# Grouped-query attention and a gated MLP: one fixed order for all engines, six score bursts a batch, a ring of PSUM banks, and DMA transposes

## The chip, the cores and the metric

The kernel runs on one NeuronCore of a Trainium2 chip. The metric is the time of one execution in microseconds (us), as the device measures it. The spans of the profiles here are 1 to 2 us shorter than the times of the same executions.

Names: PE or TensorE is the matrix engine (PEld its weight loads), DVE is VectorE, ACT is ScalarE, POOL is GpSimd, SP issues DMAs. PSUM is the memory that matmuls write; both kernels divide it into eight banks, each of 512 fp32 numbers (2 KB) per partition. A score unit is one pair of score matmuls with its exponential, and a burst is the score matmuls of one visit, one after another.

## The reference

Eight batches, 384 positions, 16 query heads and 4 key/value heads of 64. Attention without a mask, then a feed-forward part whose gate mixes positions:

```python
scores = q @ k.T / sqrt(64)                  # each kv head serves 4 query heads
x      = softmax(scores) @ v                 # -> (8, 384, 1024)
h      = relu(x @ w_in)                      # w_in 1024 x 1024
u, v   = h[..., :512], h[..., 512:]
v_n    = (v - mean(v)) / sqrt(var(v) + 1e-6) # over the 512
v_s    = w_spatial @ v_n + b_spatial         # mixes the 384 positions
out    = (u * v_s) @ w_out                   # 512 -> 1024
```

## The kernel before

Matmuls run in fp16 with fp32 sums. Scores are computed transposed (keys on partitions), in pairs of 64-row matmuls for two kv heads; ScalarE takes the exponential; the sums of the softmax and the products with v are 32-column matmuls, four at a time on the array (in the trace twelve of them take 0.49 us, as long as three full ones of 163 ns). The reciprocal is `exp(-ln(sum))` on ScalarE, and VectorE multiplies. `mk_v`, `mk_u`, `mk_sp` and `mk_out` below are the feed-forward groups V, U, spatial and O.

The order of PE, POOL and SP was fixed by hand; that of VectorE and ScalarE was left to the scheduler. Each batch has nine visits of two score units, and after each visit as many feed-forward groups of the batch before as a time budget allows. PSUM was two pools: four banks for scores, four for all else.

```python
    ps_sc = ctx.enter_context(tc.tile_pool(name="ps_sc", bufs=2, space=bass.MemoryType.PSUM))
    ps = ctx.enter_context(tc.tile_pool(name="ps", bufs=4, space=bass.MemoryType.PSUM))
# ... (cut)
    def transpose_q(b, gp, jp):          # and the same for k: TensorE, then a VectorE copy
        # ... (cut)
                nc.tensor.transpose(pq[:, jj, t, :], q16[:, t, 2 * jp + jj, :, :].rearrange("p h d -> p (h d)"), ident16)
        nc.vector.tensor_copy(qT[b, gp][:, 2 * jp : 2 * jp + 2, :, :], pq)
# ... (cut)
    def mk_sp(b, m):
        # ... (cut)
            nc.tensor.matmul(psp[:, 0:S], bias_ones, bias_rows, start=True, stop=False)   # the bias
            for st in range(NST):
                nc.tensor.matmul(psp[:, 0:S], held["v_n", b, st][:, m * P : (m + 1) * P], wsT16[:, st, :],
                                 start=False, stop=(st == NST - 1))
            nc.vector.tensor_tensor(held["gT", b][:, m, :], psp[:, 0:S], held["uT", b][:, m, :], ALU.mult)
# ... (cut)
    VISITS = 9
    VALUES_AT = {0: (-1, 1, 1), 3: (0, 0, 0), 5: (0, 0, 1), 8: (0, 1, 0)}
    # ... (cut)
    with tc.manual_schedule(engines={PE, POOL, SP}):
        # ... (cut)
                if b < B:
                    scores(b, [2 * vi, 2 * vi + 1])
                if vi in VALUES_AT:
                    # ... (cut)
                        values(b + db, gp, quad)
                # ... (cut)
                budget += per_visit
                while queue and (b == B or done < budget):
                    t, f = queue.pop(0)
                    f()
                    done += t
```

The softmax here doesn't subtract the row's maximum and nothing guards it: scores larger than these inputs give would overflow.

Of the kernel before, what the change touches and what calls it, by code (L numbers as in the profile page):

```python
# [14 lines left out]
PE, POOL, SP = mybir.EngineType.PE, mybir.EngineType.Pool, mybir.EngineType.SP  # L15
# [3 lines left out]
def kernel(  # L19
# [11 lines left out]








    nc = tc.nc
    P = 128  # L40
# [10 lines left out]
    NGP = HKV // 2  # L51
    assert S == NST * P and DM == NKT * P and DH == 512 and D == 64 and G == 4
    assert HQ * D == DM and G * S == 3 * 512 and NST == 3 and NGP == 2
# [5 lines left out]
    wpool = ctx.enter_context(tc.tile_pool(name="wpool", bufs=1))  # L59
    stage = ctx.enter_context(tc.tile_pool(name="stage", bufs=1))  # L60
    ld = ctx.enter_context(tc.tile_pool(name="ld", bufs=1))
    qk16 = ctx.enter_context(tc.tile_pool(name="qk16", bufs=2))
    tr_sb = ctx.enter_context(tc.tile_pool(name="tr_sb", bufs=3))
    att_a = ctx.enter_context(tc.tile_pool(name="att_a", bufs=2))
    xt_pool = ctx.enter_context(tc.tile_pool(name="xt_pool", bufs=3))
    r_pool = ctx.enter_context(tc.tile_pool(name="r_pool", bufs=3))
    moe_sb = ctx.enter_context(tc.tile_pool(name="moe_sb", bufs=2))
    moe_v = ctx.enter_context(tc.tile_pool(name="moe_v", bufs=6))
    small = ctx.enter_context(tc.tile_pool(name="small", bufs=4))
    out_pool = ctx.enter_context(tc.tile_pool(name="out_pool", bufs=3))  # L70

    ps_sc = ctx.enter_context(tc.tile_pool(name="ps_sc", bufs=2, space=bass.MemoryType.PSUM))
    ps = ctx.enter_context(tc.tile_pool(name="ps", bufs=4, space=bass.MemoryType.PSUM))
# [15 lines left out]
    loaded = {}  # L89

    def load_k(b):
        k32 = ld.tile([P, HKV, NST * D], FP32, name=f"k32_{b}", tag="k32")
        nc.sync.dma_start(k32, k[b].rearrange("g (p t) d -> p g (t d)", t=NST))
        loaded["k32", b] = k32

    def load_v(b):
        v32 = ld.tile([P, HKV, NST * D], FP32, name=f"v32_{b}", tag="v32")
        nc.sync.dma_start(v32, v[b].rearrange("g (p t) d -> p g (t d)", t=NST))
        loaded["v32", b] = v32

    def load_q(b, gp, pieces=1):
        q32 = ld.tile([P, 2 * G, NST * D], FP32, name=f"q32_{b}_{gp}", tag=f"q32_{gp}")
        n = 2 * G // pieces
        for i in range(pieces):
            h0 = gp * 2 * G + i * n
            nc.sync.dma_start(
                q32[:, i * n : (i + 1) * n, :],
                q[b, h0 : h0 + n].rearrange("h (p t) d -> p h (t d)", t=NST),
            )
        loaded["q32", b, gp] = q32  # L110

    def cast_k(b, engine):
        k16 = qk16.tile([P, NST, HKV, D], FP16, name=f"k16_{b}", tag="k16")
        engine.tensor_copy(k16, loaded["k32", b].rearrange("p g (t d) -> p t g d", t=NST))  # L114
        loaded["k16", b] = k16

    def cast_v(b, engine):
        v16 = qk16.tile([P, HKV, NST, D], FP16, name=f"v16_{b}", tag="v16", bufs=3)
        engine.tensor_copy(v16.rearrange("p g t d -> p g (t d)"), loaded["v32", b])
        loaded["v16", b] = v16  # L120

    def cast_q(b, gp, engine):
        q16 = qk16.tile([P, NST, G, 2, D], FP16, name=f"q16_{b}_{gp}", tag=f"q16_{gp}")
        q32 = loaded["q32", b, gp]
        for half in range(2):
            engine.tensor_copy(
                q16[:, :, :, half, :],
                q32[:, half * G : (half + 1) * G, :].rearrange("p j (t d) -> p t j d", t=NST),
            )
        loaded["q16", b, gp] = q16  # L130

    def load_batch(b, first):
        load_k(b)
        load_q(b, 0)
        cast_k(b, first)
        cast_q(b, 0, first)
        load_v(b)
        load_q(b, 1)
        cast_v(b, nc.gpsimd)
        cast_q(b, 1, nc.gpsimd)  # L140
# [6 lines left out]
    bias_rows = cst.tile([P, S], FP16, name="bias_rows")  # L147
    bias_ones = cst.tile([P, P], FP16, name="bias_ones")
    w_in16 = wpool.tile([P, NKT, DFF], FP16, name="w_in16")
    w_out16 = wpool.tile([P, NDT, DM], FP16, name="w_out16")  # L150
    wsT16 = wpool.tile([P, NST, S], FP16, name="wsT16")

    def load_consts():
        make_identity(nc, ident)
        nc.vector.tensor_copy(ident16, ident)  # L155
        nc.vector.memset(ones32, 1.0)
        nc.vector.memset(eps_t, eps_ln)
        nc.vector.memset(bias_rows, 0.0)
        nc.vector.memset(bias_ones, 0.0)
        nc.vector.memset(bias_ones[0:1, :], 1.0)  # L160
        nc.vector.memset(bias_ones[32:33, :], 1.0)

    def load_bias():
        b32 = cst.tile([1, S], FP32, name="b32")
        lo32 = cst.tile([1, NST, P], FP32, name="lo32")
        nc.sync.dma_start(b32, moe_b_spatial.rearrange("(a s) -> a s", a=1))
        b_tp = b32.rearrange("a (p t) -> a t p", t=NST)
        hi = bias_rows[0:1, :].rearrange("a (t p) -> a t p", t=NST)
        lo = bias_rows[32:33, :].rearrange("a (t p) -> a t p", t=NST)
        nc.vector.tensor_copy(hi, b_tp)  # L170
        nc.vector.tensor_tensor(lo32, b_tp, hi, ALU.subtract)
        nc.vector.tensor_copy(lo, lo32)

    def load_w_in(c0, c1):

        for gp in range(2):
            for half in range(2):
                for quad in range(2):
                    r0 = (gp * 2 * G + half * G + 2 * quad) * D
                    rows = moe_w_in[r0 : r0 + 2 * D, c0:c1].rearrange(  # L180
                        "(jq jj r) n -> jq r jj n", jq=2, jj=2
                    )
                    kc = gp * 4 + quad * 2
                    for jq in range(2):
                        i = half * 2 + jq
                        nc.gpsimd.dma_start(  # L186
                            w_in16[32 * i : 32 * (i + 1), kc : kc + 2, c0:c1], rows[jq]
                        )
# [8 lines left out]
    def load_ws():  # L197
        ws32 = stage.tile([P, NST, S], FP32, name="ws32", tag="ws32", bufs=1)
        nc.sync.dma_start(ws32, moe_w_spatial.rearrange("(p tt) s -> p tt s", tt=NST))
        ws16 = stage.tile([P, NST, NST, P], FP16, name="ws16", tag="ws16", bufs=1)  # L200
        for tt in range(NST):
            nc.vector.tensor_copy(  # L202
                ws16[:, tt, :, :], ws32[:, tt, :].rearrange("p (s t) -> p t s", t=NST)
            )
        loaded["ws16"] = ws16

    def transpose_ws(st):
        ws16 = loaded["ws16"]
        psw = ps.tile([P, NST, P], FP16, name=f"psw_{st}", tag="ps")
        for tt in range(NST):  # L210
            nc.tensor.transpose(psw[:, tt, :], ws16[:, tt, st, :], ident16)
        nc.vector.tensor_copy(wsT16[:, st, :].rearrange("p (t q) -> p t q", t=NST), psw)


    kT, qT, aT, xT = {}, {}, {}, {}

    def transpose_k(b):
        k16 = loaded[("k16", b)]
        pk = ps.tile([P, NGP, NST, P], FP16, name=f"pk_{b}", tag="ps")
        for gp in range(NGP):  # L220
            for t in range(NST):
                nc.tensor.transpose(  # L222
                    pk[:, gp, t, :],
                    k16[:, t, 2 * gp : 2 * gp + 2, :].rearrange("p g d -> p (g d)"),
                    ident16,
                )
        kT[b] = tr_sb.tile([P, NGP, NST, P], FP16, name=f"kT_{b}", tag="kT")
        nc.vector.tensor_copy(kT[b], pk)

    def transpose_q(b, gp, jp):  # L230
        q16 = loaded[("q16", b, gp)]
        if jp == 0:
            qT[b, gp] = tr_sb.tile([P, G, NST, P], FP16, name=f"qT_{b}_{gp}", tag=f"qT_{gp}", bufs=2)
        pq = ps.tile([P, 2, NST, P], FP16, name=f"pq_{b}_{gp}_{jp}", tag="ps")
        for jj in range(2):
            for t in range(NST):
                nc.tensor.transpose(
                    pq[:, jj, t, :],
                    q16[:, t, 2 * jp + jj, :, :].rearrange("p h d -> p (h d)"),
                    ident16,  # L240
                )
        nc.vector.tensor_copy(qT[b, gp][:, 2 * jp : 2 * jp + 2, :, :], pq)

    def scores(b, units):
        scs = []
        for u in units:
            gp, c, t = u // 9, (u % 9) // 3, u % 3
            sc = ps_sc.tile([P, 2, 512], FP32, name=f"sc_{b}_{u}", tag="sc")
            rhs = qT[b, gp].rearrange("p j t q -> p (j t q)")
# [19 lines left out]
    def values(b, gp, quad):  # L269
# [23 lines left out]
        for jj in range(2):  # L293
# [4 lines left out]
            )  # L298


    held = {}

    def mk_v(b, st):
        def f():
# [203 lines left out]
```

## Time and profile before

Two runs took 301.69 and 302.72 us. From the page of the profile: the span, the busy time of each engine, and the engines' shares of the chain of waits (the chain of work that ended last, followed back from the end; "issue" in it is time for which the profile shows no wait, and SPq is SP's instruction queue).

```profile
span 301.4 us, 5836 instructions
PE 269.2 (89%) x2457; PEld 125.4 (42%) x2457; DVE 161.7 (54%) x310; ACT 184.3 (61%) x249; POOL 53.2 (18%) x82
...
PE 69%; ACT 16%; DMA 6%; DVE 4%; issue 2%; SPq 1%; POOL 0%; DVEq 0%
```

The next view gives busy time in four stretches, cut where a batch's first score matmul starts: before batch 1, batch 1, batches 2 to 6, batch 7 with the tail. PEclk is the granted clock of TensorE, as a share of full speed; the DMA share is the summed time of all DMA packets over that of 16 engines. It passes 1 where packets overlap.

```profile
core 0: us, PE busy (x) PEld busy (x) DVE busy (x) ACT busy (x) POOL busy (x), PEclk, DMA share, GB/s
0.00:35.05 35.05, 18.52 (x192) 9.00 (x193) 15.63 (x30) 20.51 (x25) 20.00 (x41) 0.90 0.99 240
35.05:72.38 37.33, 34.36 (x314) 16.08 (x313) 19.19 (x38) 23.40 (x32) 8.69 (x12) 0.95 0.38 94
72.38:243.39 171.01, 163.87 (x1533) 75.73 (x1532) 94.24 (x181) 114.26 (x155) 24.54 (x30) 1.00 0.36 116
243.39:301.40 58.01, 52.41 (x425) 24.60 (x424) 32.64 (x63) 26.16 (x38) 0.00 (x0) 0.99 0.16 65
```

A steady batch takes 171.01 / 5 = 34.2 us. PE is busy for 96% of that, ScalarE for 67%, VectorE for 55%. The timeline of one steady batch shows what PE does and what its steps cost: start, duration, engine, line, operation, output and inputs.

```profile
99.90 0.51 PE L237 MATMUL pq_0_0_1339<-ident_102,q_3_0_1062 128*128 128x128 f16 x6
...
101.97 1.03 PE L387 MATMUL po_1_1_1361<-w_out_108,gT_1281 128*128 128x512 f16 x4
...
102.93 0.39 PE L252 MATMUL sc_16_1368<-qT_1_1031,kT_831 64*128 64x512 f16 x2
...
103.15 0.38 PE L252 MATMUL sc_17_1371<-qT_1_1031,kT_831 64*128 64x512 f16 x2
...
103.46 0.67 PE L280 MATMUL sums_1_0_1376<-aT_1_1197,ones_103 128*32 128x384 f16 x12
```

A record lasts longer than the step to the next one: the matmuls of O take 379 ns each, and a group of four starts 0.86 us after the group before it (101.11 and 101.97). So what is counted here is the step from start to start. Between records of matmuls that follow each other the median step is 216 ns for 512 columns, 163 ns for 384, 56 ns for a transpose (its copy, on VectorE, takes 0.55 us for each 128x768), about 0.22 us for a pair of 64-row score matmuls (102.93 to 103.15) and 0.49 us for twelve 32-column ones. Where the shape of the array changes (a mode change, below), a step is longer: from O to scores 312 ns (216 would do), from scores to sums 306, from the 32-column groups to full ones 258 (163 would do). That is some 95 ns for each change.

So a batch is, in us: scores 4.0, sums and values 5.9, V 5.2, U 5.2, spatial with bias 2.6, O 5.2, transposes 1.7, together 29.8; mode changes 22 x 0.095 = 2.1; the remaining 2.3 of 34.2 are waits.

### The profile page before, as it was taken

Reading aid. Unit: us, or ns where it says so; the run is one execution under the profiler, and the core shown is the slowest. Engines: PE = TensorE matmul, PEld = TensorE weight load, DVE = VectorE, ACT = ScalarE, POOL = GpSimd, SP = SyncE. Lnnn points to the kernel's source line nnn. Section 1 sums busy time; section 2 is a strip of 40 time slices with the busy share of each in tenths; the row PEclk is TensorE's granted clock in tenths of the full one; section 3 lists DMA queues with packets and bytes.
Section 4 is the critical chain, followed back from the end, with each engine's and each line's share of the span. In section 5 each row is a group of like instructions: output and inputs, shape, how many; then the busy total and the mean of one; then the engine's idle time right before and its main releaser. Section 6 shows DMA issues by size and latency. Waiting matters only on the chain.

```text
span 301.4 us, 5836 instructions
## 1 busy us (share of the span) xinstructions
PE 269.2 (89%) x2457; PEld 125.4 (42%) x2457; DVE 161.7 (54%) x310; ACT 184.3 (61%) x249; POOL 53.2 (18%) x82
## 2 busy tenths in 40 slices
PE   0576879899899989999899989999899989999993
PEld 0332434444445434444345434444344434444551
DVE  3437325564465554665455654755455754645574
ACT  1396965657776585566786485566876485675300
POOL 0666952000140003200050001500051000000000
PEclk9977979999999999999999999999999999999998
DMA  7999991003660219103570219103480111003105
GB/s 216 315 287 218 116 254 35 2 0 142 197 188 2 119 52 318 37 0 141 164 222 0 103 50 316 56 2 140 137 251 0 70 73 72 0 2 139 72 0 209
DMA packets 31852, 35.57 MB, mean 118 GB/s; under 512 B 1489, under 2 KB 28114, under 8 KB 31826
## 3 DMA queue, kind: packets, MB, share of 16 engines
q1 hardware_dynamic: 28722, 32.05, 32.4%
q0 software_dynamic: 3104, 3.15, 6.8%
q8 instruction: 19, 0.31, 0.4%
q14 instruction: 7, 0.06, 0.1%
HBM read 25.76 MB, written 12.58 MB: 127 GB/s over the span
## 4 chain that ended last, share of the span: by engine, by line
PE 69%; ACT 16%; DMA 6%; DVE 4%; issue 2%; SPq 1%; POOL 0%; DVEq 0%
DMA ws_316<-in_moe_w_spatial_dram 3%; DMA q_0_1_135<-in_q_dram 3%; ACT aT_1_720 L265 1%; ACT aT_0_2385 L265 1%; ACT aT_0_969 L265 1%; ACT aT_1_335 L265 1%; ACT aT_0_1441 L265 1%; ACT aT_0_489 L265 1%; PE pv_0_588 L311 1%; ACT aT_0_3329 L265 1%; ACT aT_0_1913 L265 1%; ACT aT_0_2857 L265 1%; ACT aT_1_2613 L265 1%; ACT aT_1_3539 L265 1%; ACT aT_1_3085 L265 1%
## 5 line engine op out<-in xcount | busy, mean ns | idle before, releaser
L348 PEld LDWEIGHTS <-w_in_107 128*128 128x128 f16 x256 | 23.9, 98 | 21.6 <-issue 6.9
L186 POOL DMA_DIRECT2D w_in_107<-in_moe_w_in_dram x32 | 17.1, 543 | 5.3 <-DMA w_in_107<-in_moe_w_in_dram 5.3
L280 PEld LDWEIGHTS <-ones_103 128*32 128x32 f16 x384 | 7.4, 96 | 15.1 <-issue 13.3
L222 PE MATMUL pk_177<-ident_102,k_0_128 128*128 128x128 f16 x6 | 0.8, 303 | 9.6 <-DVE ident_102 L155 9.6
L265 ACT ACTIVATE aT_0_209<-sc_0_203 128x1024 f16<-128x1024 f32 x1 | 1.0, 1024 | 10.3 <-PE sc_0_203 L252 10.3
L114 POOL CAST k_3_1060<-k_3_1056 128x768 f16<-128x768 f32 x1 | 0.8, 827 | 33.0 <-DVE stats_0_1086 L321 33.0
L252 PEld LDWEIGHTS <-kT_184 64*128 64x128 f16 x36 | 2.1, 99 | 9.4 <-issue 8.9
L114 POOL CAST k_6_2476<-k_6_2472 128x768 f16<-128x768 f32 x1 | 0.8, 827 | 27.7 <-DMA k_6_2472<-in_k_dram 27.7
L114 POOL CAST k_5_2004<-k_5_2000 128x768 f16<-128x768 f32 x1 | 0.8, 827 | 26.6 <-DMA k_5_2000<-in_k_dram 26.6
L114 POOL CAST k_7_2948<-k_7_2944 128x768 f16<-128x768 f32 x1 | 0.8, 827 | 25.4 <-DMA k_7_2944<-in_k_dram 25.4
L114 POOL CAST k_4_1532<-k_4_1528 128x768 f16<-128x768 f32 x1 | 0.8, 827 | 25.1 <-DMA k_4_1528<-in_k_dram 25.1
L280 PEld LDWEIGHTS <-v_0_138 128*32 128x32 f16 x96 | 2.9, 106 | 4.4 <-issue 3.2
L202 DVE CAST ws_318<-ws_316 128x384 f16<-128x384 f32 x3 | 1.9, 671 | 5.2 <-DMA ws_316<-in_moe_w_spatial_dram 5.2
L222 PEld LDWEIGHTS <-k_0_128 128*128 128x128 f16 x6 | 0.6, 133 | 9.5 <-DVE k_0_128 L114 5.2
L364 PEld LDWEIGHTS <-bias_ones 128*128 128x128 f16 x32 | 3.1, 97 | 3.5 <-issue 2.3
L311 PEld LDWEIGHTS <-xt_271 128*128 128x128 f16 x24 | 2.7, 116 | 3.5 <-issue 1.6
L387 PEld LDWEIGHTS <-gT_3623 128*128 128x128 f16 x24 | 2.2, 98 | 3.5 <-issue 0.7
L387 PEld LDWEIGHTS <-gT_3895 128*128 128x128 f16 x24 | 2.3, 98 | 3.0 <-DVE gT_3895 L373 0.5
L387 PEld LDWEIGHTS <-gT_2697 128*128 128x128 f16 x24 | 2.2, 97 | 3.0 <-DVE gT_2697 L373 0.6
L387 PEld LDWEIGHTS <-gT_1753 128*128 128x128 f16 x24 | 2.2, 97 | 3.0 <-DVE gT_1753 L373 0.6
L387 PEld LDWEIGHTS <-gT_2225 128*128 128x128 f16 x24 | 2.2, 97 | 3.0 <-DVE gT_2225 L373 0.6
L387 PEld LDWEIGHTS <-gT_1281 128*128 128x128 f16 x24 | 2.2, 97 | 3.0 <-DVE gT_1281 L373 0.6
(1168 smaller groups left out, 804.7 us busy)
## 6 DMA issues: line engine op xcount, KB each, us to landing
w_in_107<-in_moe_w_in_dram POOLq DMA_DIRECT2D x32, 64.0 KB, 5.4
w_out_108<-in_moe_w_out_dram POOLq DMA_DIRECT2D x2, 512.0 KB, 7.4
q_0_0_125<-in_q_dram SPq DMA_DIRECT2D x2, 384.0 KB, 5.4
q_0_1_135<-in_q_dram SPq DMA_DIRECT2D x2, 384.0 KB, 8.3
q_1_0_247<-in_q_dram SPq DMA_DIRECT2D x1, 768.0 KB, 6.2
q_1_1_256<-in_q_dram SPq DMA_DIRECT2D x1, 768.0 KB, 8.5
q_2_0_571<-in_q_dram SPq DMA_DIRECT2D x1, 768.0 KB, 12.9
q_2_1_580<-in_q_dram SPq DMA_DIRECT2D x1, 768.0 KB, 8.2
```

The lines of the kernel that those rows point to most:

```text
L114: engine.tensor_copy(k16, loaded["k32", b].rearrange("p g (t d) -> p t g d", t=NST))
L186: nc.gpsimd.dma_start(w_in16[32 * i : 32 * (i + 1), kc : kc + 2, c0:c1], rows[jq])
L202: nc.vector.tensor_copy(ws16[:, tt, :, :], ws32[:, tt, :].rearrange("p (s t) -> p t s", t=NST))
L222: nc.tensor.transpose(pk[:, gp, t, :], k16[:, t, 2 * gp : 2 * gp + 2, :].rearrange("p g d -> p (g d)"), ident16,)
L252: nc.tensor.matmul(sc[:, half, :], kT[b][lo:hi, gp, t, :], rhs[lo:hi, c * 512 : (c + 1) * 512], start=True, stop=True,)
L265: nc.scalar.activation(aT[b, gp][:, t, :, c * 512 : (c + 1) * 512], sc, AF.Exp, scale=scale)
L280: nc.tensor.matmul(dst[32 * i : 32 * (i + 1), 0:S], weights(t, half), a[:, t, half, j * S : (j + 1) * S], start=(t == 0), stop=(t == NST - 1),
L311: nc.tensor.matmul(pv, xt[:, kc, st * P : (st + 1) * P], w_in16[:, kc, DH:DFF], start=(kc == 0), stop=(kc == NKT - 1),)
L348: nc.tensor.matmul(pu[:, 0:S], w_in16[:, kc, mu * P : (mu + 1) * P], xT[b][:, kc, :], start=(kc == 0), stop=(kc == NKT - 1),)
L364: nc.tensor.matmul(psp[:, 0:S], bias_ones, bias_rows, start=True, stop=False)
L387: nc.tensor.matmul(po, gT[:, m, tt * P : (tt + 1) * P], w_out16[:, m, half * 512 : (half + 1) * 512], start=(m == 0), stop=(m == NDT - 1),)
```

## The change

Its intent: fix the order of all engines; have fewer changes of the array's shape (six bursts of three score units in place of nine of two, and the softmax sums and values of two head groups together); take the transposes off TensorE (a DMA transposes, batch 0 excepted); fuse the gate (the bias becomes an addition on VectorE, and ReLU and gate one VectorE instruction; V's ReLU moves from ScalarE to VectorE); let every group use every PSUM bank (the free one used longest ago); start sooner; and do the first half of batch 0's V and U in batch 0. The feed-forward is also spread over two batches: V and half of spatial and U one batch later, the other half and O two batches later. The core of the diff:

```diff
-    ps_sc = ctx.enter_context(tc.tile_pool(name="ps_sc", bufs=2, space=bass.MemoryType.PSUM))
-    ps = ctx.enter_context(tc.tile_pool(name="ps", bufs=4, space=bass.MemoryType.PSUM))
+    psp = ctx.enter_context(tc.tile_pool(name="psp", bufs=1, space=bass.MemoryType.PSUM))
+    banks = psp.tile([P, 8, 512], FP32, name="banks")
+    def take1():
+        x = min((i for i in range(8) if not busy[i]), key=lambda i: used[i])
+        mark(True, (x,))
+        return x
 # ... (cut: take2 takes a pair in the same way; touch() marks a bank as free after its last reader)
+    def turn_q_dma(b, gp):
+        nc.sync.dma_start_transpose(
+            new_qT(b, gp).rearrange("p a b c -> p (a b) c"),
+            T["q16", b, gp].rearrange("p j t h d -> p (j t h d)"),
+        )
 # ... (cut)
-            nc.tensor.matmul(psp[:, 0:S], bias_ones, bias_rows, start=True, stop=False)
+        nc.vector.tensor_tensor(vs, f32(x, S), bias_tp, ALU.add)
 # ... (cut)
+        nc.vector.scalar_tensor_tensor(
+            T["gT", b][:, mu, :], src, 0.0, T["vs", b, mu], op0=ALU.max, op1=ALU.mult
+        )
 # ... (cut)
+    def C(b, gp, quads):                 # softmax sums, reciprocals, values, normalisation
+        for qd in quads:
+            sums(b, gp, qd)
+        for qd in quads:
+            recip(b, gp, qd)
+        for qd in quads:
+            for jj in range(2):
+                value(b, gp, qd, jj)
+                norm(b, gp, qd, jj)
+
+    def visit(b, vi):
+        us = [3 * vi, 3 * vi + 1, 3 * vi + 2]
+        if b < B:
+            for u in us:
+                score(b, u)
+            for u in us[:2]:
+                expo(b, u)
+        if vi == 1 and b > 1:
+            C(b - 1, 1, (0, 1))
+        if vi == 4 and b < B:
+            C(b, 0, (0, 1))
+        if b < B:
+            expo(b, us[2])
+        f, g = b - 1, b - 2
+        run(*{
+            0: [("sp", g, 2), ("U", g, 2), ("sp", g, 3), ("U", g, 3)],
+            1: [("O", g, 0)],
+            2: [("V", f, 0), ("st", f, 0), ("O", g, 1), ("V", f, 1), ("st", f, 1)],
+            3: [("O", g, 2), ("V", f, 2), ("st", f, 2), ("O", g, 3), ("rs", f, 0), ("vn", f, 0)],
+            4: [("O", g, 4)],
+            5: [("O", g, 5), ("sp", f, 0), ("U", f, 0), ("sp", f, 1), ("U", f, 1)],
+        }[vi])
 # ... (cut: loads, casts on POOL and DMA transposes of batch b + 1, in visits 0 to 3)
-    with tc.manual_schedule(engines={PE, POOL, SP}):
+    with tc.manual_schedule():
 # ... (cut: batch 0 written out, with half V and U groups "VA" and "UA" between its scores)
```

## The prediction

> **What bounds the kernel now.** TensorE. The page gives PE 89% busy, VectorE 54%, ScalarE 61%, DMA engines mostly idle after 40 us. In the chain of waits PE has 69%, ScalarE 16%. In the timeline a batch repeats every 34.2 us from 76 to 247 us at granted clock 1.00. Start-to-start steps of matmuls there: 216 ns (512 columns), 162 ns (384), 58 ns (a transpose), 223 ns for a pair of 64-row score matmuls, 0.49 us for twelve 32-column ones. Summed over one batch: scores 4.0, sums and values 5.9, V 5.2, U 5.2, spatial 2.6 (0.65 of it the bias matmul), output 5.2, transposes 1.8: 29.9 us. The other 4.3 us are mode changes and waits: a step from or to scores, or out of the 32-column matmuls, takes 255-314 ns where 162-216 would do, about 95 ns lost some 24 times (2.3 us). [...] About 2 us are waits on ScalarE and VectorE results and PSUM buffers. Outside the steady part: 41 us until the first feed-forward matmul, with PE waiting (9.6 us at start, later for ScalarE, the late normalisation of batch 0 behind the spatial-weight cast, and loads), and 28 us after the last scores.
>
> **What the change does, per steady batch.** PE loses the transposes (-1.8) and bias matmuls (-0.65); six bursts of three scores and paired values leave about 14 mode changes (-1.0). VectorE loses five copies (5 x 0.55) and the ReLU of U, gains the bias addition (4 x 0.55) and V's ReLU (3 x 0.69, off ScalarE's 3 x 0.60): about even. PE's floor becomes 27.4 + 1.3 = 28.7 us. I expect 1.5-2.5 us of waits to remain: three score pairs take six of eight banks, so after each values group the next burst waits for reciprocal and normalisation (ScalarE does two exponentials, four 0.5 us steps, then the third exponential, 4.9 us for a 4.7 us visit), and the variance step holds ScalarE's exponentials once a batch. Period: 30.5-31 us against 34.2.
>
> DMA gains 30 blocks of 128x128 a batch. [...] some 15 us of slack lie between cast and use.
>
> **Sum (estimate).** Batch 1's scores start at 34 us (35 before): transposes start earlier, but loads[...] and the Pool queue's weight issues bind. Half of batch 0's V and U (5.2 us) moves into that idle time. Batch 1 then carries no older work, and ScalarE binds it: 18 x 0.92 + 6 x 0.52 + 0.5 = 20.5 us. Batches 2-7: 6 x 30.5 = 183. The tail grows, because output work of batch 6 now lies there: PE 29.5 + 1.5 waits + 4.5 last copy and store. Total about 34 + 20.5 + 180 (6 x 30, between floor and expectation) + 35 = 269.5.
>
> Predicted: 269 us, range 257 to 285. Chances: faster 0.87, same 0.05, slower 0.08.
>
> **What would show it.** Right: period 29.5-31 us in the timeline, no transposes on PE after batch 0, PE the largest part of the chain; first exponential at about 9 us (12.3 before); score bursts waiting up to 1 us after values groups; landing of transposes under 8 us. Wrong: score bursts of a new batch waiting for transposed q or k; transposes filling the DMA engines and delaying output stores; batch 1 starting after 38 us.
>
> **What would make it wrong.** Slow DMA transposes, above all; the ring turning into a wait longer than I sum; VectorE's fixed order holding normalisation behind output copies.

The sum comes to 34 + 20.5 + 180 + 35 = 269.5 us.

## The result, and the profile after

The two runs took 276.50 and 278.89 us, median 277.69, against 302.21. The ratio is 0.918, with a 95% interval of 0.907 to 0.929. (The medians quoted here give 0.919.) Four more runs on another occasion gave 278.62 and a ratio of 0.9195 (0.913 to 0.926). The page:

```profile
span 277.1 us, 5400 instructions
PE 250.4 (90%) x2206; PEld 114.2 (41%) x2206; DVE 159.5 (58%) x304; ACT 171.0 (62%) x227; POOL 55.8 (20%) x87
...
PE 63%; DMA 11%; ACT 10%; DVE 9%; issue 3%; POOL 2%; SPq 0%; DVEq 0%
```

The same four stretches, cut at the same events, of the kernel after:

```profile
0.00:39.84 39.84, 24.12 (x203) 9.74 (x203) 14.27 (x31) 22.80 (x27) 24.61 (x48) 0.95 1.04 210
39.84:62.31 22.47, 17.88 (x170) 7.48 (x170) 12.21 (x24) 19.78 (x26) 7.18 (x10) 0.93 1.08 216
62.31:212.79 150.48, 148.46 (x1353) 68.21 (x1352) 92.37 (x175) 105.05 (x140) 23.97 (x30) 1.00 0.64 165
212.79:277.10 64.31, 59.95 (x483) 28.77 (x482) 40.65 (x75) 23.42 (x34) 0.00 (x0) 1.00 0.19 75
```

| stretch | before, us | after, us | difference |
|---|---|---|---|
| before batch 1's scores | 35.05 | 39.84 | +4.8 |
| batch 1 | 37.33 | 22.47 | -14.9 |
| batches 2 to 6 | 171.01 | 150.48 | -20.5 |
| batch 7 and tail | 58.01 | 64.31 | +6.3 |
| span | 301.4 | 277.1 | -24.3 |

Batch 1 and the tail belong together: output and spatial work that batch 1 carried before now runs one batch later, and so the tail has more of it. The two and the start give -3.8 us together. Most of the gain, 20.5 of 24.3 us, is the steady batches: their period is 30.36 us from batch 3 on, and 29.06 in batch 2, where two of batch 0's U tiles are half done.

The timeline of one such period, of the kernel after (152.08 to 182.44 us):

```profile
152.08 0.82 PE L280 MATMUL banks<-qT,kT 64*128 64x512 f16 x6
...
159.85 1.96 DVE L337 TENSOR_TENSOR xT<-banks,rec 128x384 f16<-128x384 f32 x4 [2.68 <-ACT rec L319]
...
161.28 1.18 PE L280 MATMUL banks<-qT,kT 64*128 64x512 f16 x6
...
171.87 1.44 PE L301 MATMUL banks<-aT,ones 128*32 128x384 f16 x24
...
173.53 2.13 PE L301 MATMUL banks<-aT,v 128*32 128x384 f16 x48 [0.22 <-ACT aT L292]
...
175.36 1.96 DVE L337 TENSOR_TENSOR xT<-banks,rec 128x384 f16<-128x384 f32 x4 [1.30 <-ACT rec L319]
...
176.57 1.39 PE L280 MATMUL banks<-qT,kT 64*128 64x512 f16 x6
```

A burst of three score pairs takes 0.82 us when its banks are free. The bursts that follow a values group (161.28 and 176.57) take 1.18 and 1.39: the normalisation on VectorE (159.85 to 161.81, and 175.36 to 177.32) has still to read the banks. That is 0.36 + 0.57 = 0.93 us a batch. The sums of visit 4 take 1.44 where those of visit 1 take 1.16, and its values wait for an exponential.

With the same steps as before, PE's work is 27.5 us a batch (29.8 less 1.7 of transposes and 0.65 of bias), the mode changes are 14 x 0.095 = 1.3, and 1.6 us are waits. So the 3.8 us by which the period fell are 1.7 of transposes, 0.65 of bias, 0.8 of mode changes and 0.7 of waits. The first two are tested below by taking them back (e8, e6). The other two are accounts: the 0.8 is a count times a step, the 0.7 is what is left over. Which part of the change removed those waits (the fixed order of VectorE and ScalarE, the ring, the fused gate, the spread over two batches) was not tested one by one.

The DMA takes over the transposes. Of the DMA view, packets before and after, and the issues of the kernel after (count, median us from issue to landing):

```profile
DMA packets 31852, 35.57 MB, mean 118 GB/s; under 512 B 1489, under 2 KB 28114, under 8 KB 31826
```

```profile
DMA packets 60953, 42.91 MB, mean 155 GB/s; under 512 B 30337, under 2 KB 57089, under 8 KB 60929
...
qT<-q SPq DMA_TRANSPOSE x14, 4.2
...
kT<-k SPq DMA_TRANSPOSE x7, 3.4
```

Their median landing takes 3.4 and 4.2 us, and the busy share of the DMA engines in steady batches goes from 0.36 to 0.64. In steady batches PE's list of waits names no DMA, so no score burst waited there for a transposed q or k.

What went against the forecast is the start. The chain of waits before batch 1, kernel after (start, length, what):

```profile
25.07 8.44 DMA w_in<-in_moe_w_in_dram
...
33.79 0.53 POOL w_in L134
34.33 1.60 POOL q L211 x2
35.93 0.02 issue
35.95 3.76 DMA qT<-q
39.70 0.14 issue
39.84 0.62 PE banks L280 x2
```

Batch 1's first query half is cast on POOL. There it stands behind 24 weight loads, whose issues wait for loads of the same weights to land (over all 32 of them POOL's list of waits has 7 such waits, 10.1 us in all); then its transpose follows. PE had nothing to do from 32.5 to 39.8 us (its idle time before these scores is 7.36 us). The experiments test this reading and the account of the steady batches.

### The profile page after: what moved, and what is told of

Read it like the earlier page. It is cut to its first block, busy times and chain, and to the rows that moved or that the text cites. A ratio compares the mean times of both kernels' runs of the same rounds, so it can differ in the third digit from the quotient of the medians. Undisturbed runs are those within 1.5% of the kernel's fastest.

```text
span 277.1 us, 5400 instructions
## 1 busy us (share of the span) xinstructions
PE 250.4 (90%) x2206; PEld 114.2 (41%) x2206; DVE 159.5 (58%) x304; ACT 171.0 (62%) x227; POOL 55.8 (20%) x87
## 4 chain that ended last, share of the span: by engine, by line
PE 63%; DMA 11%; ACT 10%; DVE 9%; issue 3%; POOL 2%; SPq 0%; DVEq 0%
PE banks L109 46%; PE banks L280 9%; DMA w_in<-in_moe_w_in_dram 8%; PE banks L301 8%; ACT aT L292 6%; DVE xT L337 3%; DVE bn L394 2%; ACT rec L319 2%; DVE v_r L381 2%; POOL w_in L134 2%; DMA q<-in_q_dram 1%; DMA qT<-q 1%; ACT rec L317 1%; ACT rstd L399 1%; POOL q L211 1%
## 5 line engine op out<-in xcount | busy, mean ns | idle before, releaser
L292 ACT ACTIVATE aT<-banks 128x1024 f16<-128x1024 f32 x144 | 137.9, 1022 | 51.6 <-PE banks L280 51.0
L280 PE MATMUL banks<-qT,kT 64*128 64x512 f16 x288 | 50.1, 398 | 11.4 <-DMA qT<-q 7.4
L337 DVE TENSOR_TENSOR xT<-banks,rec 128x384 f16<-128x384 f32 x64 | 31.6, 552 | 43.4 <-ACT rec L319 43.1
L109 PE MATMUL banks<-w_out,gT 128*128 128x512 f16 x192 | 48.6, 380 | 0.0
L109 PE MATMUL banks<-xT,w_in 128*128 128x384 f16 x256 | 47.4, 326 | 0.0
L109 PE MATMUL banks<-w_in,xT 128*128 128x512 f16 x192 | 46.0, 380 | 1.2 <-DVE xT L337 0.6
L301 PE MATMUL banks<-aT,v 128*32 128x384 f16 x768 | 35.7, 335 | 3.1 <-ACT aT L292 3.1
L457 DVE COPY osb<-banks 128x512 f32<-128x512 f32 x48 | 32.5, 681 | 8.2 <-PE banks L109 8.1
L109 PEld LDWEIGHTS <-w_in 128*128 128x128 f16 x256 | 24.6, 98 | 17.1 <-issue 1.0
L211 POOL CAST q<-q 128x768 f16<-128x768 f32 (+1 forms) x29 | 22.8, 816 | 26.7 <-DMA q<-in_q_dram 20.5
L134 POOL DMA_DIRECT2D w_in<-in_moe_w_in_dram x32 | 17.1, 542 | 10.2 <-DMA w_in<-in_moe_w_in_dram 10.1
```

What stands on the lines that cost most here:

```text
L109: nc.tensor.matmul(dst, w, m, start=(i == 0), stop=(i == n - 1))
L134: nc.gpsimd.dma_start(w_in16[32 * i : 32 * (i + 1), kc : kc + 2, c0:c1], rows[jq])
L211: engine(T["q16", b, gp][:, j0 : j0 + n, :, half, :], T["q32", b, gp][:, half * G + j0 : half * G + j0 + n, :].rearrange("p j (t d) -> p j ...
L280: nc.tensor.matmul(banks[:, x + half, :], T["kT", b][lo:hi, t, gp, :], rhs[lo:hi, c * 512 : (c + 1) * 512], start=True, stop=True,)
L292: nc.scalar.activation(T["aT", b, gp][:, t, :, c * 512 : (c + 1) * 512], banks[:, x : x + 2, :], AF.Exp, scale=scale)
L301: nc.tensor.matmul(dst[32 * i : 32 * (i + 1), :], weights(t, half), a[:, t, half, j * S : (j + 1) * S], start=(t == 0), stop=(t == NST - 1),)
```

## The experiments

Twelve kernels, all with the reference's result, all against the kernel before in the same rounds, four timed runs each. Periods are of batches 3 to 6 in the trace, as differences of the first score matmul of each batch. "Changed kernel" is the kernel after.

### The changed kernel again (e0_after_again)

No edit.

> The changed kernel again, unedited, to stand beside the experiments on the same chip. Expected 275 to 279 us and, in the trace, batch 1's scores starting at 39.8 us again, a period of 30.3 to 30.4 us for batches 3 to 6.

Measured: 278.62 us, period 30.36, batch 1's scores at 38.70, batch 2's at 63.98 (first trace: 39.84 and 62.31). So steady batches are exact from trace to trace, while the start varies by 1 to 2 us. Six more experiments below (e4, e5, e7, e8, e9, e11) leave the code up to batch 1's scores as it is; there these start at 37.58 to 38.34. So the 39.84 of the first trace is the latest of eight. In batch 1 of this run TensorE's granted clock was 0.75 on average, against 0.93 in the other: it stands at 0.50 not only for the first 6 us, but again from 55.0 to 61.8 us. (The 48 value matmuls at 56.08 take 4.03 us there, against 2.13 in the steady batch shown above.)

### Batch 1's query cast off POOL, and first on POOL (e1_q0_cast_vector, e2_q0_cast_pool_first)

```diff
 # e1
-        cast_q(1, 0, pool, 0)
-        cast_q(1, 0, pool, 1)
+        cast_q(1, 0, vec, 0)
+        cast_q(1, 0, vec, 1)
 # e2: the same two casts, on POOL, moved up
         load_q(1, 0)
+        cast_q(1, 0, pool, 0)
+        cast_q(1, 0, pool, 1)
         load_w_in(1, DH, DFF)
```

> The cast of batch 1's first query half moves from the Pool engine, where it stands behind 24 weight-load issues, to VectorE. Theory A (the 7.4 us wait before batch 1's scores is the Pool engine's order[...]): the transpose is issued at about 26 us in place of 36, batch 1's scores start at 32.5 to 34 us in place of 39.8, and the run is 5 to 7 us shorter than the unedited changed kernel. Rival B (the DMA engines are full until about 38 us, so the transposes or the weights of the feed-forward become the next wait): the start of batch 1 moves but the start of batch 2 (62.3 us) moves by less than 2.5 us, and so does the run's time.

> The same cast stays on the Pool engine but is placed before the second half of the weight-load issues. Theory A (order, not the engine's speed): batch 1's scores start as early as in the VectorE version, within 1.5 us. But the Pool engine then waits for the query load before it issues 16 more weight loads; if those loads bind (rival B), the second half of the first feed-forward (batch 1) waits for weights and the run gains less than the VectorE version, by 1 us or more.

Measured: 277.44 and 277.27 us, against 278.62 of the changed kernel; the intervals of the ratios overlap (0.910 to 0.923, 0.910 to 0.922, 0.913 to 0.926), so three rounds don't settle a gain. In the traces batch 1's scores start at 36.09 in both, and batch 2's at 59.3 and 59.7, so 2.6 to 3.8 and 2.7 to 4.7 us sooner than in the two traces of the changed kernel. (Against all eight traces with the same start, batch 1 is 1.5 to 3.8 us sooner.) The expected 32.5 to 34 didn't come. The chain of waits of e1 shows the next wait:

```profile
25.20 10.75 DMA qT<-q
35.95 0.14 issue
36.09 1.47 PE banks L280 x6
```

The transpose is issued at 25.2 as expected, but lands 10.75 us later, where the median of all is 4.2: from 25 to 36 us the mean busy share of the DMA engines is 1.29 in this run, so packets overlap there. In e2 it is issued at 25.05 and lands after 10.9 us. So both readings hold in part: POOL's order was the first wait, and the DMA the one behind it. What in the DMA holds the transpose was not separated: besides POOL's weight loads, three earlier transfers of the same SP queue are still under way when it is issued in e1, and land at 28.06 (spatial weights), 29.47 (bias) and 31.24 us (the transpose of k).

### Batch 0's V and U not in halves (e3_no_halves)

```diff
-        run(("VA", 0, 0))     # and VA 1, 2 and UA 0 to 3: all seven half groups out
```

> Batch 0's V and U are computed whole in batch 1, as for all other batches, in place of a first half in batch 0. It moves 5.2 us of TensorE work (12 matmuls of 216 ns and 16 of 162 ns) from batch 0 into batch 1 and 2. Theory A (batch 1 is bound by ScalarE, 20.5 us of its work against 13.6 us of TensorE's, and only U's last two tiles lie in batch 2): the run is 0 to 2 us longer. Rival B (TensorE's work in batch 1 counts fully): 4 to 6 us longer.

Measured: 280.77 us, so 2.1 more than the changed kernel by the medians, but the intervals of the ratios overlap (0.9215 to 0.9312 against 0.9128 to 0.9263), so the size is not settled. What the traces show is batch 2: its period is 30.35 in place of 29.16, about the 2 x 0.65 us of two half U tiles; batch 1's end does not move (62.86 against 62.31 and 63.98). So 5.2 us of PE work moved into batch 0 are worth 1 to 2. That ScalarE, busy for 20.0 of the 24.6 us of batch 1 here, is what bounds that batch fits, but was not tested. The result is near theory A's upper edge and far from B.

### Transposes back on TensorE, twice (e4_pe_transposes, e8_pe_transposes_spread)

```diff
 # e4: in visits 3, 4 and 5, at the end of each (lines joined)
-                turn_k_dma(n)
-                turn_q_dma(n, 0)
-                turn_q_dma(n, 1)
+            if vi == 3: turn_k_pe(n, 0, vec); turn_k_pe(n, 1, vec)
+            if vi == 4: turn_q_pe(n, 0, (0, 1), vec); turn_q_pe(n, 0, (2, 3), vec)
+            if vi == 5: turn_q_pe(n, 1, (0, 1), vec); turn_q_pe(n, 1, (2, 3), vec)
 # e8: k and the first query half between the items of visit 5,
 #     the second half between the items of the next batch's visit 0
```

> The transposes of q and k for batches 2 to 7 go back to TensorE (30 of 58 ns a batch, 1.74 us) with six VectorE copies (2.9 us); batch 1 keeps the DMA. Theory A (TensorE bounds the steady batches, and DMA transposes are off the critical path): the period of batches 3 to 6 grows from 30.4 to 32.0 to 32.8 us and the run by 9 to 14 us. Rival B (ScalarE and VectorE chains or DMA traffic set the period, TensorE has room): the period grows by less than 0.8 us. The mean busy share of the DMA engines falls clearly either way.

> As the run with the transposes of batches 2 to 7 back on TensorE, but placed in visits 5 and 0, between feed-forward groups, where VectorE has room (about 2.5 us busy of 5), in place of visits 3 to 5 directly ahead of score bursts. That run lost 25 us, 3 to 5 us a batch. Theory A (1.74 us a batch is TensorE's own work, and the rest of that loss was the placement: copies queued behind VectorE's other work held the PSUM banks that the next score burst needed): the period of batches 3 to 6 is 32.0 to 32.6 us and the run 9 to 13 us longer than the changed kernel. Rival B (a ring of eight banks has no room for transposes anywhere): 33 us or more, as before.

Measured: e4 303.42 us, ratio 1.001, with steady batches of 33.6 to 35.2 us. It gives back all of the gain, far more than both theories. The timeline says why:

```profile
186.97 0.50 PE L245 MATMUL banks<-ident,k 128*128 128x128 f16 x6
...
187.41 0.60 PE L280 MATMUL banks<-qT,kT 64*128 64x512 f16 x4
...
188.59 0.37 PE L280 MATMUL banks<-qT,kT 64*128 64x512 f16 x1 [0.58 <-DVE osb L457]
...
189.92 0.62 DVE L250 COPY kT<-banks 128x384 f16<-128x384 f16 x2
...
190.33 0.37 PE L280 MATMUL banks<-qT,kT 64*128 64x512 f16 x1 [1.36 <-DVE kT L250]
```

The transposes of k at 186.97 took two banks, and their copies stood on VectorE behind statistics, an output copy and the normalisation of v, until 189.92. The score burst needs three pairs of the eight banks, so PE waited. This was my placement, not the transposes. e8 has the same work where VectorE has room: 289.15 us, period 32.03, 1.67 more than the changed kernel, and 10.5 us a run (medians). That is theory A: 30 x 56 ns = 1.7 us. The windows view of one e8 period also shows what DMA transposes cost the DMA engines:

```profile
126.92:158.95 32.03, 31.63 (x304) 15.48 (x304) 20.39 (x40) 21.02 (x28) 4.81 (x6) 1.00 0.39 125
```

0.39 x 32.03 = 12.5 us of DMA time a batch against 0.64 x 30.1 = 19.3 in the changed kernel. So 30 blocks of 32 KB (0.98 MB) take about 6.8 us of all 16 engines, some 145 GB/s. That is an estimate from the difference of packet times of two kernels, taken while other transfers run, so it is no bandwidth. The changed kernel's trace has a stretch in which nothing but transposes moves, just before batch 1 (columns as in the four stretches):

```profile
36.95:39.70 2.75, 0.00 (x0) 0.00 (x0) 0.00 (x0) 0.00 (x0) 2.75 (x5) 0.50 1.05 193
```

There they move 193 GB/s at a share of 1.05.

### Score bursts split (e5_bursts_split)

```diff
-            for u in us:
+            for u in us[:2]:
                 score(b, u)
 # the third score and its exponential come later, between the feed-forward items of the visit
+        cut = {0: 2, 1: 0, 2: 3, 3: 3, 4: 0, 5: 3}[vi]
+        run(*items[:cut])
+        score(b, us[2])
+        expo(b, us[2])
+        run(*items[cut:])
```

> The third score pair of each visit is issued later, between feed-forward items, which gives ten more changes of tiling mode a batch. Theory A (each change costs about 95 ns on TensorE): the period grows by 0.7 to 1.2 us and the run by 5 to 9 us. Rival B (what three-score bursts cost or save is the wait for PSUM banks): the period stays or falls, because the third pair finds its banks free and the waits inside the bursts after values groups (0.9 us a batch) go away.

Measured: 280.43 us, period 30.85. The trace has 24 mode changes a batch in place of 14, so 10 x 0.095 = 0.95 us more of PE's time; but the period grows by only 0.49, so the waits fell by about 0.46. Both theories are half right. Long bursts save mode changes and pay part of it back in waits for banks.

### The bias on TensorE (e6_bias_matmul)

```diff
-            [
+            [(bias_ones, bias_rows.rearrange("p (t q) -> p t q", t=NST))]
+            + [
                 (T["v_n", b, st][:, m * P : (m + 1) * P], wsT[:, :, st, :])
-        nc.vector.tensor_tensor(vs, f32(x, S), bias_tp, ALU.add)
+        nc.vector.tensor_copy(vs, f32(x, S))
```

> The bias of the spatial projection is again a matmul (4 a batch, 162 ns each, 0.65 us), and VectorE copies in place of adding, at the same length. Theory A (TensorE-bound): the period grows by 0.6 to 0.8 us, the run by 4 to 6 us. Rival B (waits absorb it): under 2 us.

Measured: 283.12 us, period 31.01, so +0.65 a batch. The run is 4.5 us longer by the medians of two occasions, and 3.8 by the ratios to the kernel before (0.9321 and 0.9195). Theory A: 4 x 163 ns. These matmuls count in full in a steady batch.

### V's ReLU on ScalarE (e11_relu_v_scalar)

```diff
-    V_ON_ACT = False
+    V_ON_ACT = True
```

> The changed kernel with the ReLU of V back on ScalarE (3 of 0.60 us a batch) in place of VectorE (3 of 0.69 us). Theory A (neither engine bounds a steady batch, only their order does): the period moves by at most 0.4 us either way and the run by less than 3 us. Rival B (the exponentials on ScalarE, whose order is fixed, get late behind V's matmuls): the period grows by 0.5 us or more.

Measured: 277.02 us, period 30.26. Theory A: moving 2 us from one side engine to the other changes 0.1 us.

### Output groups right after the values (e7_more_after_values)

```diff
-            1: [("O", g, 0)],
-            2: [("V", f, 0), ("st", f, 0), ("O", g, 1), ("V", f, 1), ("st", f, 1)],
+            1: [("O", g, 0), ("O", g, 1)],
+            2: [("V", f, 0), ("st", f, 0), ("V", f, 1), ("st", f, 1)],
-            4: [("O", g, 4)],
-            5: [("O", g, 5), ("sp", f, 0), ...],
+            4: [("O", g, 4), ("O", g, 5)],
+            5: [("sp", f, 0), ...],
```

> Two output groups (O 1 and O 5, 0.87 us each) move one place earlier, so that each follows a values group directly and the next score burst comes 0.87 us later after it. Theory A (the bursts after values groups wait for the normalisation to free their PSUM banks, 0.9 us a batch): the bursts go back to 0.8 us each, the period falls by 0.6 to 0.9 us and the run by 3 to 6 us. Rival B (the wait moves to the next place): the period stays within 0.2 us.

Measured: 272.59 us, ratio 0.898 (0.893 to 0.904), period 29.43, so 0.93 less. The bursts after values groups:

```profile
188.93 0.82 PE L280 MATMUL banks<-qT,kT 64*128 64x512 f16 x6
...
203.87 0.82 PE L280 MATMUL banks<-qT,kT 64*128 64x512 f16 x6
```

They are 0.82 us again, and the period fell by just what they had waited. No work was removed: two groups of 0.86 us that did not need those banks were put where PE had waited for them. This version beats both kernels: 0.898 / 0.9195 = 0.977 of the changed kernel, and the intervals don't touch.

### The variance step later (e9_late_variance)

On top of e7:

```diff
-            3: [("O", g, 2), ("V", f, 2), ("st", f, 2), ("O", g, 3), ("rs", f, 0), ("vn", f, 0)],
-            4: [("O", g, 4), ("O", g, 5)],
+            3: [("O", g, 2), ("V", f, 2), ("st", f, 2), ("O", g, 3)],
+            4: [("vn", f, 0), ("O", g, 4), ("O", g, 5)],
         if vi == 4 and b < B:
+            run(("rs", b - 1, 0))
             C(b, 0, (0, 1))
```

> The version with O 1 and O 5 moved, and in it the two ScalarE steps of the variance come after the first two exponentials of the next visit in place of ahead of them, and the three normalisations of v after that visit's values. Theory A (ScalarE's exponentials of visit 4 wait for VectorE's variance, which holds TensorE for the value banks, 0.5 us a batch): the period falls from 29.43 to 28.8 to 29.1 us, the run by 2 to 4 us to 269 to 271. Rival B (the later normalisation of v makes the spatial matmuls wait): the period stays at 29.4 or grows.

Measured: 278.59 us, period 30.19. The wait of the values for an exponential is gone from the trace, as theory A has it, but a longer one came:

```profile
206.02 1.45 DVE L405 TENSOR_SCALAR v_n<-v_r,mv,rstd 128x512 f16<-128x512 f32 x3
...
207.38 1.28 DVE L457 COPY osb<-banks 128x512 f32<-128x512 f32 x2
...
208.12 0.65 PE L109 MATMUL banks<-wsT,v_n 128*128 128x384 f16 x3 [1.00 <-DVE osb L457]
```

The normalisation of v now stands on VectorE ahead of the output copies, and the spatial matmuls wait a microsecond for what follows it. Rival B. The sums of visit 4 still take 1.44 us in both e7 and e9, so the variance step isn't what holds them. In the changed kernel their second group starts at 172.64, and an output copy, which stands behind V's statistics on VectorE, ends at 172.59; in e9 the two times are 201.90 and 201.85. So it looks as if they wait for that copy's bank. Moving the copy ahead was not tried, so that stays open.

### Batch 1's first transposes on TensorE (e10_first_transposes_pe)

On top of e9: e1's cast on VectorE, and k and the first query half of batch 1 transposed on TensorE in batch 0.

```diff
-        turn_k_dma(1)
-        turn_q_dma(1, 0)
+        turn_k_pe(1, 0, vec); turn_k_pe(1, 1, vec)
 # ... and between half groups of batch 0:
+        turn_q_pe(1, 0, (0, 1), vec)
+        turn_q_pe(1, 0, (2, 3), vec)
```

> That version, and batch 1's k and first query half are cast on VectorE and transposed on TensorE in batch 0, where TensorE waits for ScalarE, in place of DMA transposes that queue with the loads (from 25.2 to 36 us in the run with the cast on VectorE). Theory A (with the cast on VectorE, the DMA engines full of loads are what holds batch 1's first transposes): batch 1's scores start at 32.5 to 34 us and batch 2's about 2 us earlier than with the cast alone. Rival B (the weights of the first feed-forward bind): batch 1 starts early but batch 2's start stays at 59 to 60 us. Run 266 to 270 us under A.

Measured: 275.00 us, 3.6 less than e9, with the same period. Batch 1 starts at 36.08 and batch 2 at 59.05: the first is no earlier than in e1 and e2, the second about as early. PE no longer waits for a DMA there; but it now waits 2.45 us in batch 0 for the cast of batch 1's k, which comes late on VectorE, and so batch 0 itself is longer. My placement again. What the start would be with neither wait is open.

## Why the prediction was right or wrong

The measured 277.69 us lies in the range of 257 to 285, the direction was right, and the mechanism of the steady batches was too. The middle, 269, was 8.7 us low; in the trace, where the sum of 269.5 stands against 277.1, nearly all of it lies before batch 2.

- **What bounds it.** Right: TensorE. The bias matmul's 0.65 us and the transposes' 1.7 count in full, as e6 and e8 show. (Not all does: of the 0.95 us that e5 adds, 0.49 reach the period.)
- **Mode changes.** Right in kind. "about 95 ns lost some 24 times" is 22 times in the trace; 14 after is right. The steps were 306 to 312 ns for 216, and 258 for 163; what TensorE does in that time was not shown. e5 adds that a saved change isn't a saved wait: ten more cost 0.95 us of PE's time (an estimate, 10 x 95 ns) and 0.49 of the period's.
- **Period "30.5-31 us".** Measured 30.36; the sum then used 30. "1.5-2.5 us of waits to remain": 1.6.
- **The ring's wait.** Right in place and size ("waiting up to 1 us after values groups": 0.36 and 0.57), and e7 shows the cause by removing it. The second part, "the variance step holds ScalarE's exponentials once a batch", was seen (the chain of waits runs through it), but taking it away by e9's order made things worse.
- **DMA transposes.** That they would be fast enough rested on no trace. It held in steady batches: twelve blocks landed in 4.2 us (median), at most 350 ns each, where the transposes of k and of the first query half were issued 15.4 and 13.9 us ahead of the scores that read them (136.67 and 138.15 for 152.08). They moved 193 GB/s with nothing else moving, and about 145 by the estimate from e8. In steady batches no score burst waited for them, so it didn't matter there; at the start it did.
- **"Batch 1's scores start at 34 us".** This step failed: 39.8 in the trace of the result, 5.8 us of the 7.6 missed there, and 37.6 to 39.8 in eight traces. A start after 38 us stood in the prediction's own list of what would show it wrong. I had named the loads and POOL's weight issues as the limit, but did not follow one operand, batch 1's first query half, through POOL's queue and then a transpose behind and beside loads. e1 and e2 show that the first wait hides a second: with the cast out of POOL's way the scores start at 36.1, not at 34, and wait for the transpose.
- **Batch 1 "20.5 us".** Measured 22.5 and 25.3. ScalarE is the busiest engine (19.8 of 22.5 us), but it waits 1.8 us for the variance (VectorE does an addition and a ReLU for each halved V tile), and TensorE came out of its wait at a lower granted clock. In the trace of the result PE is idle from 32.5 us, and its granted clock stands at 0.50 from 36.0 to 42.9 us. In e0 it falls again at 55.0 us, when PE's wait before that had lasted only since 53.6. What sets the clock was not shown. How much of the 2.0 us each of these cost was not tested.
- **"Half of batch 0's V and U (5.2 us) moves into that idle time."** True, but worth only 1 to 2 us (e3, not clear of noise).
- **Tail of 35 us** after batch 7's 30: 33.9 measured.

Added up for the trace of the result, in us: start +5.8, batch 1 +2.0, six batches +0.9, tail -1.1; together the 7.6 between 269.5 and the span of 277.1.

## What to carry to other kernels

On an engine that is nearly always busy, cost a change by that engine's own steps, and then look at what each group leaves behind: a group that frees its buffers late needs independent work after it, and moving two such groups was worth more (0.93 us a batch) than the fused bias (0.65). A side engine with 40% of its time free (VectorE here, busy for 58% of the span) can still hold the busy one, by the order of its queue: transposes put where VectorE was full cost 25 us, and the same transposes elsewhere 10.5. For a start-up phase follow each first operand from load to use through every queue; here an estimate that named the loads as the limit, and did not follow that operand, missed 3.6 to 5.8 us.
